# T5-bias attention and a mixture of adapters: two passes through DRAM rewritten as one hand-ordered pass over head pairs

## The chip, the cores and the metric

The kernel runs on one core of one Trainium2 chip. The metric is the device time of one execution in microseconds (us). A profiled run also gives a span, from the first to the last instruction; it is about 2 us shorter than the time. The engines are named as in the profile: PE is TensorE's matmuls, PEld its weight loads, DVE is VectorE, ACT ScalarE, POOL GpSimd, SP SyncE, which issues the DMAs that the kernels start with `nc.sync`. PEclk is the share of TensorE's full clock that was granted.

## The reference

Eight batches, eight heads, 576 tokens, head size 64. Attention with a bias that depends on the distance between query and key alone, and is constant from distance 128 on; then, per token, a mixture of eight rank-16 adapters of which the two with the largest gate logits count.

```python
scores = q @ k.T / sqrt(64) + bias_table[bucket(|i - j|)]     # per batch and head, 576 x 576
attn   = softmax(scores)                                       # over keys
x      = (attn @ v)                                            # heads side by side: 4608 x 512
logits = x @ w_gate                                            # 4608 x 8
w      = softmax of the two largest logits
out    = x + sum over the two experts e of  w_e * (x @ A[e]) @ B[e]
```

The softmax needs no maximum for numbers of this size: both kernels multiply exp(scores) by exp(bias), and get the sum of a row by appending a column of ones to the values.

## The kernel before

A scheduler orders the instructions. First a bias stage writes 40 tables of exp(bias), one per head and block of 128 keys:

```python
for h in range(H):
    for jb in range(JB):                      # 5 blocks of keys: 4 x 128 + 64
        nc.sync.dma_start(out=tmp[:P, :], in_=<a 576-wide sliding window of gext_d>)
        nc.scalar.activation(eb[:P, :], trev, ACT.Exp)         # ebias, L96
```

Then the attention stage, per head. Queries and keys come as bf16 copies through DRAM, are transposed for two heads at once, and each head takes its 64 of the 128 rows:

```python
qTs = pair["q"][lo:hi, :]                     # 64 rows
kTs = pair["k"][lo:hi, :]
for jb in range(JB):
    nc.tensor.matmul(sc[:P, n0:n1], lhsT=kTs[:, jb*128:jb*128+P], rhs=qTs[:, n0:n1], ...)  # L171
    nc.scalar.activation(e[:P, :], sc[:P, :], ACT.Exp, scale=scale)                        # L176
    nc.vector.tensor_tensor(p[:P, :], e[:P, :], ebias[(h, jb)][:P, :], op=ALU.mult)        # L179
    nc.tensor.matmul(pv[:, n0:n1], lhsT=v1[:P, jb, :], rhs=p[:P, n0:n1], ...)              # L182
nc.vector.tensor_copy(o, pv[:D, :])           # o and the row of sums go to DRAM
nc.vector.tensor_copy(rsb, pv[D:D + 1, :])
```

In L182 the values are stationary (65 columns: 64 and the ones), and the probabilities stream. When all heads are done, the sums come back from DRAM, reciprocals go out again, and a third stage runs the adapters (MoE) over 36 tiles of 128 tokens:

```python
nc.vector.tensor_tensor(xTt, xTr, dv, op=ALU.mult)             # normalise
# ... gate: about a dozen small VectorE instructions of 8 columns or 1 ...
nc.scalar.copy(ot, dl); nc.sync.dma_start(out=out[n0:n0 + 128, :], in_=ot)
```

The softmax here doesn't subtract the row's maximum and nothing guards it: scores larger than these inputs give would overflow.

## Time and profile before

The median is 626.71 us of 4 runs (622.73 to 628.53).

| stage | about | busiest | granted clock |
|---|---|---|---|
| bias tables | 0 to 70 us | waits for table DMAs | |
| attention | 90 to 495 us | TensorE | 0.50 for most of it |
| round trip and MoE | 495 to 620 us | VectorE | 0.56 |

The first lines are from the page of before: busy time of each engine with its share of the span, and then the span in 40 slices, each digit being a tenth.

```profile
PE 453.0 (73%) x1960; PEld 181.3 (29%) x1960; DVE 326.4 (53%) x949; ACT 283.9 (46%) x537; POOL 193.1 (31%) x431
PE   0000895768899999999999999999999404555554
DVE  0000453237555656656565655656566417888884
ACT  0021674557554545555455555555555203333333
PEclk9999999999655555555555555555555556565556
```

TensorE has two long rows of nines in the middle. Under them the clock is at five tenths. The next view of before is busy time by stretch: the stretch and its length, busy us and number of instructions of each engine, granted clock, DMA share and GB/s.

```profile
150.00:155.00 5.00, 5.00 (x39) 2.48 (x39) 4.89 (x12) 4.07 (x7) 3.66 (x8) 1.00 1.10 183
165.00:170.00 5.00, 4.88 (x22) 1.69 (x22) 1.83 (x4) 1.85 (x4) 1.86 (x4) 0.50 0.76 221
190.00:300.00 110.00, 107.08 (x431) 40.00 (x431) 64.86 (x132) 59.44 (x96) 37.24 (x77) 0.50 0.60 136
500.00:620.00 120.00, 57.74 (x360) 34.05 (x360) 85.46 (x468) 39.82 (x144) 45.95 (x81) 0.56 0.82 202
```

In both stretches TensorE is busy all the time, but in the first it finishes 39 matmuls, and in the second 22. Busy time cannot tell the two apart; the granted clock does. The 1.00 that the profile shows before 149 us is not a measurement: the first clock record of the trace is at 149 us, time without a record counts as full clock, and the matmuls before it have the durations of half clock (the 512-column score matmuls 598 ns in the mean from 70 to 130 us, and 602 from 160 to 175 us, where the records show 0.50). So a mean clock can be too high: 8 of the 28 runs of before in the later calls are listed at 0.94 to 0.97 and still took 624 to 629 us. Their first record may have come later still; their traces were not kept, so this is not shown.

From the groups by line of before, with the mean duration in ns after the comma, and from its waits (us in total, times, longest):

```profile
L176 ACT ACTIVATE e<-sc 128x576 bf16<-128x576 f32 x256 | 161.8, 648 | 154.2 <-PE sc L171 116.9 <-PE pv L182 17.0 <-DVE p L179 9.8
L171 PE MATMUL sc<-pTq,pTk 64*128 64x512 bf16 x256 | 148.6, 595 | 15.4 <-ACT e L176 14.1 <-ACT pTk L149 0.7
L179 DVE TENSOR_TENSOR p<-e,ebias 128x576 bf16<-128x576 bf16 x256 | 105.2, 444 | 116.7 <-ACT e L176 98.7 <-ACT ebias L96 17.8
```

```profile
ACT ebias L96 <- DMA eb_tmp<-gext_d: 62.7, 23, 25.4
PE zl L248 <- DMA dv<-recips_d: 22.7, 1, 22.7
```

ScalarE idles 154 us before its exps and VectorE 117 us before its multiplies, mostly for the engine ahead of them, while TensorE idles 15 us before its large score matmuls: attention is TensorE's. The other two lines are the price of the two detours through DRAM.

### The profile page before, as it was taken

How to read it: one execution, taken by the hardware profiler on the slowest of the kernel's cores; microseconds unless marked ns; L12 is line 12 of the kernel's file. 1: busy time of each engine (PE TensorE's matmuls, PEld its weight loads, DVE VectorE, ACT ScalarE, POOL GpSimd, SP SyncE). 2: the span in 40 equal slices, each digit the busy share in tenths (PEclk: the TensorE clock that was granted, in tenths of full speed). 3: DMA queues.
4: the chain of work that ended last, by engine and by line, in shares of the span. 5: the costliest groups of instructions: out<-in, count | busy, mean ns of one | idle time of the engine just before them, and what ended most of it. 6: DMA issues, size and time to landing. Idle time of an engine off the chain costs nothing. (4 is left out here: it accounts for less than half of the span.)

```text
span 620.8 us, 7660 instructions
## 1 busy us (share of the span) xinstructions
PE 453.0 (73%) x1960; PEld 181.3 (29%) x1960; DVE 326.4 (53%) x949; ACT 283.9 (46%) x537; POOL 193.1 (31%) x431
## 2 busy tenths in 40 slices
PE   0000895768899999999999999999999404555554
PEld 0000331223333333333333333333333102333332
DVE  0000453237555656656565655656566417888884
ACT  0021674557554545555455555555555203333333
POOL 7040123114342423433232322323231055344420
PEclk9999999999655555555555555555555556565556
DMA  5999589669876775942222232101010089989872
GB/s 114 227 248 243 130 247 215 155 160 225 184 164 123 191 144 167 199 122 58 49 48 40 44 58 44 29 20 31 19 29 20 21 137 214 234 217 245 234 190 103
DMA packets 134388, 82.96 MB, mean 134 GB/s; under 512 B 110144, under 2 KB 115520, under 8 KB 134344
## 3 DMA queue, kind: packets, MB, share of 16 engines
q1 hardware_dynamic: 116168, 49.26, 31.2%
q0 software_dynamic: 13056, 28.48, 23.1%
q10 hardware_dynamic: 5120, 4.72, 2.4%
q8 instruction: 16, 0.26, 0.2%
q14 instruction: 28, 0.23, 0.1%
HBM read 67.93 MB, written 28.64 MB: 156 GB/s over the span
## 5 line engine op out<-in xcount | busy, mean ns | idle before, releaser
L176 ACT ACTIVATE e<-sc 128x576 bf16<-128x576 f32 (+1 forms) x320 | 201.0, 647 | 167.3 <-PE sc L171 126.1
L171 PE MATMUL sc<-pTq,pTk 64*128 64x512 bf16 (+3 forms) x640 | 209.9, 424 | 15.7 <-ACT e L176 14.3
L179 DVE TENSOR_TENSOR p<-e,ebias 128x576 bf16<-128x576 bf16 (+1 forms) x320 | 133.2, 445 | 142.5 <-ACT e L176 116.1
L171 PEld LDWEIGHTS <-pTk 64*128 64x128 bf16 (+1 forms) x640 | 56.5, 118 | 136.6 <-issue 132.8
L188 DVE CAST o<-pv 64x576 bf16<-64x576 f32 x64 | 48.0, 749 | 71.3 <-PE sc L171 58.3
L238 POOL DMA_DIRECT2D dv<-recips_d x72 | 44.1, 617 | 57.2 <-DVE lm L258 15.5
L143 PE MATMUL tpk<-ident,ntk 128*128 128x128 bf16 (+1 forms) x160 | 29.1, 284 | 38.9 <-DMA ntk<-k_bf 38.8
L96 ACT ACTIVATE ebias<-eb_tmp 128x576 bf16<-128x576 f32 (+1 forms) x40 | 26.7, 680 | 62.7 <-DMA eb_tmp<-gext_d 62.7
L192 DVE COPY rsb<-pv 1x576 f32<-1x576 f32 x64 | 48.1, 752 | 2.0
L143 PE MATMUL tpq<-ident,ntq 128*128 128x128 bf16 (+1 forms) x160 | 26.6, 287 | 24.2 <-DMA ntq<-q_bf 23.8
L193 POOL DMA_DIRECT2D sums_d<-rsb x64 | 32.4, 506 | 23.6 <-DVE rsb L192 23.6
L286 PE MATMUL ztT_ps<-ident,zt 128*128 128x128 bf16 x36 | 10.3, 287 | 40.2 <-DVE zt L281 37.4
L248 PE MATMUL zl<-AW,xTt 128*128 128x136 bf16 x144 | 22.4, 308 | 22.7 <-DMA dv<-recips_d 22.7
L244 DVE TENSOR_TENSOR xTt<-xTr,dv 128x512 bf16<-128x512 bf16 x36 | 24.9, 692 | 23.3 <-DMA xTr<-xT_d 13.7
L147 DVE COPY pTq<-tpq 128x576 bf16<-128x576 bf16 x32 | 14.6, 458 | 35.7 <-PE tpq L143 34.9
L297 ACT COPY ot<-dl 128x512 f32<-128x512 f32 x36 | 21.1, 586 | 27.0 <-PE dl L293 18.2
L143 PEld LDWEIGHTS <-ntk 128*128 128x128 bf16 (+1 forms) x160 | 13.9, 117 | 60.5 <-DMA ntk<-k_bf 39.8
L143 PEld LDWEIGHTS <-ntq 128*128 128x128 bf16 (+1 forms) x160 | 14.8, 127 | 39.7 <-issue 27.9
L290 PE MATMUL dl<-Bc,ztT 128*128 128x512 bf16 x36 | 21.0, 584 | 6.9 <-ACT ztT L288 6.6
L149 ACT COPY pTk<-tpk 128x576 bf16<-128x576 bf16 x32 | 20.0, 625 | 12.1 <-PE tpk L143 12.1
L248 PEld LDWEIGHTS <-xTt 128*128 128x128 bf16 x144 | 15.6, 138 | 23.3 <-issue 23.1
L293 PE MATMUL dl<-ident,xTt 128*128 128x128 bf16 x144 | 21.7, 302 | 0.0
(773 smaller groups left out, 519.7 us busy)
## 6 DMA issues: line engine op xcount, KB each, us to landing
eb_tmp<-gext_d SPq DMA_DIRECT2D x32, 288.0 KB, 4.0
dv<-recips_d POOLq DMA_DIRECT2D x72, 128.0 KB, 4.9
out_dram<-ot SPq DMA_DIRECT2D x36, 256.0 KB, 3.4
cb<-in_q_dram POOLq DMA_DIRECT2D x8, 576.0 KB, 6.1
q_bf<-cb SPq DMA_DIRECT2D x8, 576.0 KB, 3.7
cb<-in_k_dram POOLq DMA_DIRECT2D x8, 576.0 KB, 7.6
cb<-in_v_dram POOLq DMA_DIRECT2D x8, 576.0 KB, 8.0
k_bf<-cb SPq DMA_DIRECT2D x8, 576.0 KB, 4.5
```

The lines of the kernel that those rows point to most:

```text
L96: nc.scalar.activation(eb[:P, :], trev, ACT.Exp)
L143: nc.tensor.transpose(tp[:, jb * 128:jb * 128 + P], nt[:P, jb, :], ident[:P, :P])
L171: nc.tensor.matmul(sc[:P, n0:n1], lhsT=kTs[:, jb * 128:jb * 128 + P], rhs=qTs[:, n0:n1], start=True, stop=True)
L176: nc.scalar.activation(e[:P, :], sc[:P, :], ACT.Exp, scale=scale)
L179: nc.vector.tensor_tensor(p[:P, :], e[:P, :], ebias[(h, jb)][:P, :], op=ALU.mult)
L188: nc.vector.tensor_copy(o, pv[:D, :])
L192: nc.vector.tensor_copy(rsb, pv[D:D + 1, :])
L193: nc.gpsimd.dma_start(out=sums_d.ap()[h, b * S:(b + 1) * S], in_=rsb)
L238: nc.gpsimd.dma_start(out=dv[hs * 64:(hs + 1) * 64, :, :], in_=bass.AP(tensor=rd.tensor, offset=rd.offset + hs * N + n0, ap=[[0, 64], [2 * ...
L244: nc.vector.tensor_tensor(xTt, xTr, dv, op=ALU.mult)
L248: nc.tensor.matmul(zl, lhsT=xTt[:, c, :], rhs=AW[:, c, :], start=(c == 0), stop=(c == 3))
L293: nc.tensor.matmul(dl[:, c * 128:(c + 1) * 128], lhsT=xTt[:, c, :], rhs=ident, start=False, stop=(c == 3), skip_group_check=True)
```

## The change

The intent, in five parts:

1. One pass. A head pair goes through scores, exp, band, PV and normalisation; the MoE of the batch before is cut into pieces, one of which runs in each gap of the loop. Nothing but inputs, a small bias table and outputs touches DRAM.
2. The order is by hand: `tc.manual_schedule()`, and PV of pair i-1 stands between the scores of pair i.
3. Toeplitz band: only the blocks within 128 of the diagonal are multiplied by exp(bias - bias of the last bucket); the constant of the far columns cancels in the softmax.
4. Token-major PV: the probabilities are stationary, the values stream (65 or 130 columns), and the result has tokens on partitions, so that a reciprocal per token normalises it.
5. Scores from keys zero-padded to 128 rows, so that each matmul uses all 128 rows of the array.

The core of the diff (cut; `+` lines of the new loop):

```diff
-    nc.tensor.matmul(sc[:P, n0:n1], lhsT=kTs[:, ...], rhs=qTs[:, n0:n1], ...)    # 64 rows
+    nc.vector.tensor_copy(t[0:64, 0, :], ps[0:64, 0, :])      # L256: head 0, rows 64-127 stay zero
+    nc.vector.tensor_copy(t[64:128, 1, :], ps[64:128, 0, :])  # L257: head 1, rows 0-63 stay zero
+    nc.vector.tensor_copy(t[:, 2, :], ps[:, 1, :])            # L258: both heads' queries
+    for h in range(2):
+        kh = t[:, h, g * 128:(g + 1) * 128]
+        nc.tensor.matmul(sc[:, h*512:(h+1)*512], lhsT=kh, rhs=t[:, 2, :], ...)           # L268
+        nc.tensor.matmul(sc[:, 1024+h*64:1088+h*64], lhsT=kh, rhs=tt[:, hp, 2, 0:64], ...)  # L270
+    nc.scalar.activation(p, sc[:, :1152], ACT.Exp, scale=scale)                          # L282
+    nc.vector.tensor_tensor(pm[:, :, q0:q1], pm[:, :, q0:q1], Mh[...], op=ALU.mult)      # L296, band
+    nc.tensor.matmul(acc[:, qb, h, :], lhsT=p[:, o:o+128], rhs=vn[:, g, 2*hp+h, :], ...)    # L317
+    nc.vector.reciprocal(rc, acc[:, :, :, D])
+    nc.vector.tensor_tensor(x[:, 0:3, ...], acc[:, :, :, :D], rc..., op=ALU.mult)        # L355
...
+    for g in range(5):
+        sc = qk(i, g); softmax_exp(i, g, sc)
+        if g == 0: transposes(i + 1)
+        if g == 1: norm_main(i - 1, pv_main(i - 1))
+        if g == 2: norm_rest(i - 1, pv_rest(i - 1))
+        if g in (0, 3, 4) and queue: queue.pop(0)()            # one piece of the MoE
+        band(i, g)
```

In PSUM, where its matmuls write, the kernel keeps two score buffers and two accumulator buffers (`acc`); transposes, PV and all MoE pieces share the latter in turn.

## The prediction

> **What bounds it now.** The slice table and the busy times by stretch show three stages. Up to about 70 us: bias tables (ScalarE waits 62.7 us for table loads). 90 to 495 us: attention, TensorE-bound (busy 107 of 110 us between 190 and 300; ScalarE 59, VectorE 65). After that: the MoE pass, VectorE-bound (85 of 120 us), behind a DRAM round trip in which TensorE waits over 20 us.
>
> In attention the granted clock is 0.50 from 159 to 521 us, though TensorE hardly idles: 512-column matmuls start about 425 ns apart. Switching between 64-row and 128-row matmuls adds some 110 ns (535 instead of 427). Scores use 64 of 128 rows. In the MoE stage, all 128-row, the clock rises for 3.4 us after each window that a burst filled. [...]360 us of busy half clock shows that busy time is not what is counted. I read it as activity weighted by rows.
>
> **What the change does.** It removes the bias stage (40 tables become small band tables), the bf16 copies through DRAM, the sums round trip and the separate MoE pass, which now fills gaps. There remain a startup of about 20 us (loads 6 to 8 us, a chain of table DMAs of about 4 us each) and a tail of about 18 us for the last batch's MoE.
>
> Estimates per head pair (32 pairs), from durations in the trace:
> - TensorE: scores 5,248 columns, transposes 1,150, PV 41 matmuls of 65 or 130 (3,250), MoE 2,060: 11,700 columns. At half clock 9.8 us, with gaps 10.5; at full clock about 5.6.
> - VectorE: 576-element bf16 multiply 445 ns, so band multiplies 2.4 us; PSUM copies (458 ns per 576 bf16) 1.6; normalisation (749 ns per 576 fp32, small ops 155) 1.4; MoE 2.1: 7.5 us, 240 us in all.
> - ScalarE: 647 ns per 576, so 1,128 per 1,152: 5.2 us, 167 us in all.
> - DMA: 110,000 rows of 256 B at about 20 ns over 16 engines: 140 us each, hidden.
>
> **Critical path.** The bias stage except 20 us, and the MoE stage except the tail, come off it. In the loop VectorE (7.5 us) is the floor at full clock, TensorE (10.5) at half. Full-row matmuls should lift the clock when TensorE is the limit; when VectorE limits, TensorE's activity falls to about 60%, so I expect the clock to alternate, mean 0.7 to 0.8. [...]So 9.5 us per pair, 305 us, plus 38.
>
> **Predicted: 345 us, 8 in 10 between 305 and 400. Chances: faster by over 2% 0.98, within 2% 0.01, slower 0.01.**
>
> **Signs.** Right: VectorE busy about 240 us, the busiest by share (over 65%); ScalarE about 170; first exp before 20 us; no final MoE stage over 25 us; clock clearly above 0.5 in the loop; TensorE waiting for VectorE on the two-buffer accumulator. Wrong: clock 0.50 throughout with TensorE near 100% busy (then 375 to 400 us); clock 1.0 with VectorE over 85% (then about 305).
>
> **What would make it wrong.** PV matmuls bound by their weight loads[...]; the gate counting something other than rows, so that zero-padding gains nothing; gate chains on VectorE waiting behind a 1.1-us exp on ScalarE; the software DMA queue (up to 1,024 rows per transfer) delivering late, so that batches start with a stall.

The sum: 7.5 us of VectorE work per pair, brought to 9.5 us by a term for hand-offs and one for the clock; 32 x 9.5 = 305 us, and with 20 us of start and 18 of tail 343, put as 345. That the clock would alternate at an activity of 60%, with a mean of 0.7 to 0.8, was the estimate; before does not show it.

"The gate" is there whatever sets the granted clock. The rises in the MoE stage are four in the clock records of before, of 3.41 us each, at 521.2, 555.4, 572.4 and 606.6 us; in the 3.4 to 3.5 us ahead of each, TensorE was busy for 2.95 to 3.16 us. The 20 ns are the mean of the 18,432 packets of 256 bytes in before's trace (20.1).

## The result, and the profile after

The changed kernel takes 272.65 us (272.60 to 272.88, 4 runs) against 626.71 us. The ratio is 0.4382, with a 95% interval of 0.4352 to 0.4412; ratios are the mean time of one kernel's fast runs over that of the other's in the same rounds, so not quite the ratio of the medians. Executions over 1.5% slower than the fastest of the same kernel are left out of the means. The time lies below the predicted range of 305 to 400 us.

The same lines of the page, after:

```profile
PE 192.0 (71%) x2704; PEld 131.3 (48%) x2704; DVE 224.0 (83%) x707; ACT 165.6 (61%) x174; POOL 117.2 (43%) x155
PE   0020778887788777888798578987787778978852
DVE  3402699999989898998999898989998889989972
ACT  2000599867678676775697667776696667758200
PEclk9999999999999999999999999999999999999975
```

There is one stage. VectorE has the nines now, and the clock is full from its first record, at 31.7 us, to 260 us. By stretch, after:

```profile
50.00:100.00 50.00, 39.92 (x598) 28.15 (x596) 45.93 (x149) 36.44 (x40) 26.27 (x32) 1.00 1.18 93
100.00:150.00 50.00, 40.96 (x592) 28.02 (x591) 46.52 (x140) 36.32 (x37) 19.26 (x24) 1.00 1.04 106
245.00:271.00 26.00, 15.56 (x183) 9.10 (x181) 18.53 (x57) 6.96 (x9) 0.00 (x0) 0.80 0.26 92
```

VectorE is busy 46 of 50 us. From the groups by line, after:

```profile
L268 PE MATMUL sc<-kqT_188 128*128 128x512 bf16 x128 | 41.0, 388 | 18.7 <-DVE kqT_188 L258 13.0 <-ACT p_1135 L282 0.7 <-ACT p_596 L282 0.7
L355 DVE TENSOR_TENSOR x<-pvA,rcA 128x384 bf16<-128x384 f32 x32 | 17.8, 557 | 1.1
L258 DVE COPY kqT_188<-kqps 128x512 bf16<-128x512 bf16 x16 | 6.8, 424 | 0.2
```

The score matmul's 388 ns is the duration that the profile gives it; in the trace the next matmul starts 215 ns after it, at a granted clock of 1.00; before, at 0.50, it was about 400 to 430. VectorE has next to no idle time before its instructions. The start of the loop is in this timeline of after (start, duration, engine, instruction, and in brackets the idle time and what ended it):

```profile
25.69 0.86 DVE L245 COPY tlT_184<-tps 64x512 bf16<-64x512 bf16 x2 [13.47 <-POOL tlT_184 L221]
28.26 0.59 PE L268 MATMUL sc<-kqT_188 128*128 128x512 bf16 x1 [12.96 <-DVE kqT_188 L258]
```

The first score matmul comes at 28.3 us: a memset of the tail tile stood behind the load issues in GpSimd's order. The loop's period, taken from the start times of the first and last normalisation, is (253.0 - 37.6) / 31 = 6.95 us per pair. After the last normalisation come 17.8 us for the last batch's MoE.

### The profile page after: what moved, and what is told of

It is laid out like the page before. It is cut to its first block, busy times and chain, and to the rows that moved or that the text cites. A ratio compares the mean times of both kernels' runs of the same rounds, so it can differ in the third digit from the quotient of the medians.

```text
span 270.8 us, 6853 instructions
## 1 busy us (share of the span) xinstructions
PE 192.0 (71%) x2704; PEld 131.3 (48%) x2704; DVE 224.0 (83%) x707; ACT 165.6 (61%) x174; POOL 117.2 (43%) x155
## 4 chain that ended last, share of the span: by engine, by line
DVE 61%; PE 15%; ACT 7%; POOL 6%; issue 6%; DMA 3%; ACTq 0%; DVEq 0%; POOLq 0%
PE pvA L317 8%; DVE x L355 5%; DVE o L464 4%; DVE x L367 3%; DMA vn_86<-in_v_dram 3%; DVE xT L384 3%; PE sc L268 3%; DVE kqT_188 L258 2%; DVE kqT_190 L258 2%; DVE kqT_188 L257 2%; DVE kqT_190 L257 2%; DVE kqT_190 L256 2%; DVE kqT_188 L256 2%; POOL qn L69 2%; DVE rcA L354 2%
## 5 line engine op out<-in xcount | busy, mean ns | idle before, releaser
L268 PE MATMUL sc<-kqT_188 128*128 128x512 bf16 x128 | 41.0, 388 | 18.7 <-DVE kqT_188 L258 13.0
L268 PE MATMUL sc<-kqT_190 128*128 128x512 bf16 x128 | 39.9, 379 | 2.7 <-ACT p_485 L282 0.7
L69 POOL DMA_DIRECT2D kn<-in_k_dram x36 | 31.1, 889 | 23.3 <-PE kqps L253 22.0
L69 POOL DMA_DIRECT2D qn<-in_q_dram x36 | 31.0, 902 | 1.0 <-DMA vn_86<-in_v_dram 1.0
L69 POOL DMA_DIRECT2D vn_86<-in_v_dram x16 | 14.0, 895 | 31.0 <-PE pvB L343 30.9
L69 POOL DMA_DIRECT2D vn_87<-in_v_dram x16 | 14.2, 903 | 30.6 <-PE pvB L343 30.6
L268 PEld LDWEIGHTS <-kqT_188 128*128 128x128 bf16 x128 | 12.7, 99 | 22.4 <-DVE kqT_188 L256 12.3
L464 DVE TENSOR_TENSOR o<-dl,x 128x512 f32<-128x512 f32 x32 | 21.8, 683 | 1.4 <-DMA out_dram<-o 0.8
L355 DVE TENSOR_TENSOR x<-pvA,rcA 128x384 bf16<-128x384 f32 x32 | 17.8, 557 | 1.1
L462 PE MATMUL dl<-Bb,zT 128*128 128x512 bf16 x32 | 12.9, 411 | 6.1 <-DVE zT L456 2.5
L270 PEld LDWEIGHTS <-kqT_188 128*128 128x128 bf16 x128 | 12.7, 99 | 9.1 <-issue 8.6
L268 PEld LDWEIGHTS <-kqT_190 128*128 128x128 bf16 x128 | 12.5, 98 | 8.2
L270 PEld LDWEIGHTS <-kqT_190 128*128 128x128 bf16 x128 | 12.5, 98 | 5.2 <-issue 4.2
L367 DVE TENSOR_TENSOR x<-pvB,rmB 128x256 bf16<-128x256 f32 x32 | 13.6, 424 | 1.1
L270 PE MATMUL sc<-tlT_184,kqT_188 128*128 128x64 bf16 x64 | 12.6, 198 | 0.0
L270 PE MATMUL sc<-tlT_184,kqT_190 128*128 128x64 bf16 x64 | 12.3, 192 | 0.0
```

The lines of the kernel that those rows point to most:

```text
L69: nc.gpsimd.dma_start(out=o, in_=src[b, h0:h1, j * 128:(j + 1) * 128, :] .rearrange("h p d -> p h d"))
L268: nc.tensor.matmul(sc[:, h * 512:(h + 1) * 512], lhsT=kh, rhs=t[:, 2, :], start=True, stop=True)
L270: nc.tensor.matmul(sc[:, 1024 + h * 64:1088 + h * 64], lhsT=kh, rhs=tt[:, hp, 2, 0:64], start=True, stop=True)
L355: nc.vector.tensor_tensor(x[:, 0:3, 2 * hp:2 * hp + 2, :], acc[:, :, :, :D], rc.unsqueeze(3).to_broadcast((128, 3, 2, D)), op=ALU.mult)
L367: nc.vector.tensor_tensor(x[:, 3:5, 2 * hp:2 * hp + 2, :], acc[:, :, :, :D], rm.unsqueeze(3).to_broadcast((128, 2, 2, D)), op=ALU.mult)
L462: nc.tensor.matmul(ps, lhsT=zT[:, t, :], rhs=Bb, start=True, stop=True)
```

## The experiments

Each kernel was run beside the kernel before on one chip; before's median in the four calls was 622.3, 622.5, 622.1 and 625.1 us. All results passed the comparison with the reference, also the one that is wrong (see there).

### Is it the rows that decide the clock? The kernel before, padded

The prediction read the gate as counting activity weighted by rows. One rival is that it counts busy time; another, array cells: rows times columns. Three edits of before tell them apart.

`b1_keys128`, one zero-padded key tile per head (cut):

```diff
-                    nc.scalar.copy(pT, tp)
+                    for hh in range(2):
+                        s = slice(hh * D, (hh + 1) * D)
+                        nc.scalar.copy(two[hh][s, :], tp[s, :])   # the other rows stay zero
-                qTs = pair["q"][lo:hi, :]
-                kTs = pair["k"][lo:hi, :]
+                qTs = pair["q"]
+                kTs = pair["k"][hh]
```

> The kernel before, with keys zero-padded to 128 rows (one padded tile per head, filled by two 64-row ScalarE copies instead of one of 128 rows). Theory R (rows): all matmuls of the attention stage now use 128 rows, so the granted clock is 1.0 through most of it, and that stage is bound by VectorE (about 3.95 us per head, 253 us in all) or ScalarE (3.9) instead of TensorE (6.4): 480 to 530 us in all. Theory C (the gate counts rows times columns of the array): PV with 65 active columns still counts half, so the clock stays at 0.5[...]: 560 to 610 us. Theory B (busy time): no change of clock, 560 to 620.

What theory C still gains here is the change of tile size: in before a 128-row matmul starts 535 ns after a 512-column one of 64 rows, where 427 ns pass between matmuls of the same rows.

Measured: 528.05 us (one run), 94 us less than before on the same chip.

`b2_v128`, the values padded from 65 to 128 columns:

```diff
-                v1 = qkp.tile([128, JB, D + 1], BF16, name="v1", tag="v1")
+                v1 = qkp.tile([128, JB, 128], BF16, name="v1", tag="v1")
-                nc.gpsimd.memset(v1[:, :, D:D + 1], 1.0)
+                nc.gpsimd.memset(v1[:, :, D:128], 1.0)
-                pv = pvp.tile([D + 1, S], FP32, name="pv", tag="pv")
+                pv = pvp.tile([128, S], FP32, name="pv", tag="pv")
```

> The kernel before, with the PV matmuls widened from 65 to 128 active columns (value tile padded with ones), scores still at 64 rows. Theory R: the rows have not changed, clock 0.5 in attention, 610 to 640 us. Theory C (rows times columns): the same weighted activity as padding the keys, about 75%, so whatever the padded-key run shows, this one shows too.

Measured: 605.83 us (one run), slightly below the expected band.

`b3_both`, both edits:

> The kernel before with both paddings. Theory R: as the padded-key run alone, 480 to 530 us at clock 1.0 in attention. Theory C: only this run of the three gets the full clock, 480 to 530 us. Theory B: clock 0.5, 560 to 620.

Measured: 529.18 us (one run), as the padded keys alone.

By stretch, 300 to 400 us: before, the padded keys, and the padded values:

```profile
300.00:400.00 100.00, 97.73 (x396) 36.73 (x395) 57.94 (x118) 53.03 (x86) 29.42 (x62) 0.50 0.23 45
```

```profile
300.00:400.00 100.00, 81.83 (x540) 42.38 (x538) 84.16 (x175) 80.12 (x132) 42.50 (x88) 0.99 0.22 47
```

```profile
300.00:400.00 100.00, 96.44 (x414) 33.79 (x414) 62.42 (x126) 57.24 (x93) 35.68 (x68) 0.55 0.22 44
```

With padded keys the clock is 0.99 here, TensorE is busy *less* (82 us instead of 98), and VectorE and ScalarE are the busiest. Padded values leave it at 0.55. This is the best stretch of the padded-key run; early on, where TensorE waited, its clock was at half as well, and it was 0.91 between 200 and 300 us:

```profile
100.00:150.00 50.00, 31.31 (x136) 13.76 (x137) 19.39 (x38) 30.72 (x50) 10.60 (x22) 0.52 0.86 198
```

For a check, the columns streamed in the stretch from 300 to 400 us were added up from the traces, weighted by active rows, and by rows and columns, as a share of what full clock could stream (2.4 columns per ns, from 512 in 215 ns):

| kernel, 300 to 400 us | granted clock | weighted by rows | by rows and columns |
|---|---|---|---|
| before | 0.50 | 0.30 | 0.21 |
| padded keys | 0.99 | 0.56 | 0.41 |
| padded values | 0.55 | 0.32 | 0.31 |
| both | 0.99 | 0.56 | 0.54 |

In these runs busy time does not decide. The two paddings did not act alike, as theory C had expected. But a level between 0.31 and 0.41 for cells would still fit these averages, as one between 0.32 and 0.56 for rows does. Single windows can tell them apart. The clock records of these traces last multiples of 3.41 us (in before 3.41, 10.24, 13.65, 30.72 and 361.81; the last one is cut off by the end), so all 17 traces were cut into windows of that length, 1,460 in all. The clock after a window was full where the row-weighted share in it was at least 0.37, and half where it was less, in all but 26 windows, and these lie between 0.32 and 0.38. (In before and after alone, 206 of 208. To guess that the clock stays as it is misses 199; at their best levels, cells miss 36 and columns without weights 135.) In the padded-key run, whose PV matmuls fill half of the columns, rows separate the windows without a miss, at 0.36, while by cells windows of 0.23 were followed by full clock and windows of 0.36 by half. So in these traces the clock goes with rows, and one level fits both rising and staying. It also fits that before stayed at half: there a 512-column matmul takes 427 ns instead of 215, so its 60% of what half clock can stream is a share of 0.30. The level is an inference, fitted to these same windows, and no run was made to test it.

### Does the new kernel need the padding? And what of changing the tile size?

`e1_scores64`, the 512-column scores over their 64 real rows:

```diff
-                nc.tensor.matmul(sc[:, h * 512:(h + 1) * 512], lhsT=kh,
-                                 rhs=t[:, 2, :], start=True, stop=True)
+                s = slice(h * 64, (h + 1) * 64)
+                nc.tensor.matmul(sc[:, h * 512:(h + 1) * 512], lhsT=kh[s],
+                                 rhs=t[s, 2, :], start=True, stop=True)
```

> The kernel after, with the 512-column score matmuls contracting over the 64 real rows instead of 128 rows of which 64 are zero; the tail scores stay at 128 rows. Nothing else changes, the copies stay. Theory R (the clock gate counts activity weighted by rows): scores are 4,096 of some 11,700 columns per pair, so the weighted activity at full clock falls from about 69% (4.9 us of 7.1) to about 57%; R with a threshold above that expects the granted clock to drop towards 0.5 and the time to go to 330 to 400 us, R with a lower threshold expects no change. Theory B (the gate counts busy TensorE time, whatever the rows): clock stays near 0.98 and the time within 272 to 285 us[...].

Measured: 344.83 us in its fast run; three others of 352.93 to 357.51 count as slow, being over 1.5% above it, and the profile is of such a run. From the page of that run:

```profile
PE   0107999999879998999989999999899999998963
PEclk9999999999995559559999855569999655589985
```

The clock alternates, in stretches of 10 to 41 us, and TensorE is the limit again. But the edit also makes TensorE change between 64-row and 128-row matmuls 16 times per pair. In the trace, at full clock, the start of a tail follows a 64-row score by 319 ns instead of 215, and the score after it by 135 instead of 28: about 105 ns for each change. To split the two, the next run has the changes without the missing rows.

`e2_tails64`, only the 64-column tails at 64 rows (both from the first head's rows, wrong; the error stayed within the tolerance of the comparison):

```diff
-                nc.tensor.matmul(sc[:, 1024 + h * 64:1088 + h * 64], lhsT=kh,
-                                 rhs=tt[:, hp, 2, 0:64], start=True, stop=True)
+                nc.tensor.matmul(sc[:, 1024 + h * 64:1088 + h * 64],
+                                 lhsT=t[0:64, 0, g * 128:(g + 1) * 128],
+                                 rhs=tt[0:64, hp, 2, 0:64], start=True, stop=True)
```

> The kernel after, with only the 64-column tail scores contracting over 64 rows (the second head's tail is computed from the first head's rows, so its result is wrong on purpose); the 512-column scores keep 128 rows. As many changes between 64-row and 128-row matmuls as in the run with 64-row scores (16 per pair, which measured some 105 ns each there, 1.7 us per pair), but the row-weighted activity is nearly that of the kernel after. Theory R: clock stays above 0.95, TensorE needs about 5.4 + 1.7 = 7.1 us per pair, level with VectorE, so 275 to 300 us; what the 64-row scores cost beyond that (352 us) is the clock. Rival D (the changes themselves, not the rows, lower the clock): clock about 0.83 and 330 to 355 us again.

Measured: 303.76 us (302.46 to 305.30), ratio to before 0.4898, clock 0.976: a little above the expected band, with the clock where theory R has it. So of the 72 us that the 64-row scores cost (344.83 - 272.65), about 31 are the changes of tile size, and the rest, about 41, goes with the clock; with the three longer runs, whose mean clock was 0.82 to 0.84, the rest would be about 50. What TensorE does at such a change these runs do not show; they put about 105 ns on it. The same term was in the kernel before (535 ns between starts instead of 427).

### When VectorE is the limit, does the clock fall?

The prediction expected it to alternate at an activity of about 60%. Two runs load VectorE further, by multiplying the columns outside the band by one, once and three times over:

```diff
+        for _ in range(1):                       # d3_full3: range(3)
+            for a0, a1 in ((0, q0), (q1, S4)):
+                if a1 > a0:
+                    nc.vector.tensor_tensor(pm[:, :, a0:a1], pm[:, :, a0:a1],
+                                            ones[:, :, 0:a1 - a0], op=ALU.mult)
```

> The kernel after, with the columns outside the band multiplied by one as well (four more bf16 multiplies per pair, 0.28 to 0.41 us each as the trace shows them, 1.1 to 1.4 us in all): what the multiply would cost without the Toeplitz band. If VectorE bounds: 272 + 32 x 1.1 to 1.4 = 306 to 318 us. TensorE's row-weighted activity then is 4.9 us of about 8.3, 59%. The prediction on record expects the clock to alternate there (mean 0.7 to 0.8); the rival, that a clock once full is kept at that activity, expects over 0.95.

Measured for `d2_full1`: 298.26 us (one run), clock 0.976, 0.99 in the loop. VectorE's busy time per pair rose from 6.41 to 7.38 us and the period from 6.95 to 7.68. The time is below the expected band: the durations rose by 1.4 us per pair, but VectorE's busy time, in which overlaps count once, by 0.97.

> The same multiplies three times over: 32 x 3.3 to 4.1 us more, 375 to 405 us at a clock that does not matter much. TensorE's activity at full clock falls to 4.9 us of about 10.8, 45%. If the full clock is kept only while activity stays over about half, the mean clock falls visibly below 0.9 here; if it is kept as long as TensorE has no long idle stretches, it stays above 0.95.

Measured for `d3_full3`: 398.24 us (one run), clock 0.819. From the stretch of 100 to 200 us, first the single, then the triple load:

```profile
100.00:200.00 100.00, 74.81 (x1041) 50.21 (x1040) 95.54 (x318) 63.18 (x69) 39.78 (x49) 1.00 0.94 91
```

```profile
100.00:200.00 100.00, 67.26 (x756) 45.39 (x754) 94.90 (x295) 46.06 (x48) 26.27 (x32) 0.82 0.67 65
```

VectorE is at 95% in both. Added up as above for 100 to 200 us, the row-weighted share of full clock and the granted clock go like this: after 0.68 and 1.00; single load 0.61 and 1.00; 64-row tails 0.59 and 0.98; triple load 0.44 and 0.82. So in these runs about 60% was enough to keep the clock (0.61 at 1.00, 0.59 at 0.98), and the kernel after was at 68% anyway. The triple load's average of 0.44 lies so near the fitted level of 0.37 that single windows can fall below it. All clock records of these traces are 0.5 or 1.0, so a mean of 0.82 is a mixture in time.

The single load also gives the worth of the band: without it the loop would take 0.73 us per pair more, some 26 us in all.

### Is VectorE's work the limit?

`d1_qcopy_act`, the query copy moved to ScalarE:

```diff
-        nc.vector.tensor_copy(t[:, 2, :], ps[:, 1, :])
+        nc.scalar.copy(t[:, 2, :], ps[:, 1, :])
```

> The kernel after, with the copy of the transposed queries out of PSUM (424 ns, once per pair) done by ScalarE instead of VectorE. If the loop is bound by VectorE's work (92% busy between 30 and 250 us): 32 times 0.42 us less, so 258 to 263 us. If it is bound by the hand-offs of the two accumulator buffers or by TensorE: within 269 to 276 us. ScalarE goes from 5.2 to about 5.8 us per pair and should not bind.

Measured: 281.06 us (280.81 to 281.83), ratio 0.4537: slower than after (0.4382), where both theories expected faster or the same. VectorE's busy time did fall, from 6.41 to 6.14 us per pair, but the period rose to 7.16. From the waits of this run between 40 and 240 us:

```profile
ACT kqT L258 <- DVE kqT L257: 16.9, 24, 1.7
PE pvA L317 <- ACT kqT L258: 15.3, 17, 1.6
```

ScalarE waits for VectorE's copy of the keys out of the same PSUM tile, and the next exp stands behind it.

`d4_qcopy_apart` gives queries and keys a PSUM tile and an SBUF tile each (cut):

```diff
-        ps = acp.tile([128, 2, S4], BF16, name="kqps", tag="acc")
+        kps = acp.tile([128, S4], BF16, name="kps", tag="acc")
+        qps = acp.tile([128, S4], BF16, name="qps", tag="acc")
...
+        nc.scalar.copy(qt, qps)
+        nc.vector.tensor_copy(t[0:64, 0, :], kps[0:64, :])
+        nc.vector.tensor_copy(t[64:128, 1, :], kps[64:128, :])
```

> Moving the query copy to ScalarE made the kernel slower (281 us), and its waits show why it may have: ScalarE waited 16.9 us in 200 for VectorE's copy of the keys out of the same PSUM tile, ahead of the next exp. Here queries and keys get a PSUM tile and an SBUF tile each, the queries are transposed first, and the ScalarE copy no longer waits for VectorE. If the wait was the reason: VectorE's work falls by 0.34 us per pair (the copy's start-to-start time) and the time to 258 to 268 us. If ScalarE's place in the order is the reason (the copy sits between two exps and the exps feed everything), or the second accumulator buffer that the pair of tiles now takes: 272 to 285 us.

Measured: 296.41 us (295.58 to 297.17), ratio 0.4781, clock 0.923: worse still. The wait for VectorE is gone, so it was not the whole reason; now ScalarE waits 41.8 us in 180 for scores that TensorE delivers late, with both accumulator buffers taken by one pair's transposes, and the clock dropped too. These two misses suggest, but do not show, that taking work off VectorE helps only if no buffer and no in-order neighbour is made to wait for it. Which of the two, the place between the exps or the second buffer, costs more was not separated.

`m1_moe_end` takes the MoE, and with it VectorE work, out of the loop without touching the order of the rest:

```diff
                 if i % HP == 0:
-                    queue += pieces(i // HP - 1)
+                    late += pieces(i // HP - 1)
...
-    for f in queue:
+    for f in late:
         f()
```

(with eight buffers for `x` instead of four).

> The kernel after with all MoE pieces run after the attention loop instead of one in each gap. If VectorE's work bounds the loop, taking about 1.9 us of 6.4 per pair out of it leaves ScalarE (5.2 us) as the limit: 5.5 to 5.9 us per pair, 35 to 45 us less; the end grows by seven batches of 11 to 12 us (what the last batch's MoE takes in the kernel after): 305 to 325 us in all. If the interleaved pieces sat in idle time of VectorE and cost the loop nothing: the loop stays at 6.9 us per pair and the time goes to 350.

Measured: 308.49 us (one run). VectorE's busy time per pair fell to 4.92 us and the period to 5.45, close to ScalarE's 4.9 us of work. The period is just below the expected 5.5 to 5.9 us, the time in the band. It fits a loop bound by VectorE, but does not prove it, since the MoE's matmuls and hand-offs left the loop as well; the cleaner evidence is `d2_full1`, which only adds VectorE work (0.97 us busy, 0.73 us of period). The interleaved MoE costs the loop 6.95 - 5.45 = 1.5 us per pair. Run at the end it takes 99 us after the last normalisation instead of 17.8:

```profile
30.00:210.00 180.00, 147.94 (x2148) 105.49 (x2178) 162.51 (x474) 160.30 (x160) 90.44 (x112) 1.00 1.10 70
210.00:306.00 96.00, 63.99 (x500) 40.39 (x504) 63.38 (x199) 2.67 (x12) 0.00 (x0) 0.54 0.29 99
```

In the second line no engine is above 67% and the clock is at 0.54: a chain of small steps that wait for each other. Interleaving is worth 36 us, though each piece takes VectorE's time in the loop.

`a1_oneacc`, one accumulator buffer instead of two (`bufs=2` to `bufs=1` for `acc_ps`):

> The kernel after with one accumulator buffer in PSUM instead of two: TensorE may fill the next one only when VectorE has read the last. If the hand-offs are a large term that two buffers hide: each of the five to six hand-offs per pair exposes a matmul group (0.3 to 1.2 us), so 2 to 3 us more per pair, 330 to 370 us. If VectorE's in-order work is so tight that the second buffer hides little: 275 to 300 us.

Measured: 380.64 us (one run), period 10.04 us, above both bands; the clock fell to 0.90 as well. The hand-offs are large, 3.1 us per pair with what the clock adds, and two buffers hide most of it: VectorE idles 6.95 - 6.41 = 0.54 us per pair.

### Two repairs

`s1_start` moves GpSimd's memsets to VectorE and issues the first batch's queries and keys ahead of its values:

```diff
-        nc.gpsimd.memset(vt, 0.0)                # and three more, and tlT's
+        nc.vector.memset(vt, 0.0)
...
-    load_v(0)
-    load_kq(0, 2, H)
+    load_kq(0, 2, H)
+    load_v(0)
```

> The kernel after with a shorter start: all memsets that GpSimd did between its load issues go to VectorE, and the remaining queries and keys of the first batch are issued before the values. In the kernel after the first copy into the tail tiles waits until 25.7 us for a memset that stands behind 15 us of load issues. Expected: first score matmul before 20 us instead of 28.3, the second pair's loads the next wait at about 21 us, 263 to 268 us in all. If the loads' landing is what bounds the start: 269 to 273.

Measured: 267.73 us (267.44 to 267.77), ratio 0.4321. The first score matmul starts 11.6 us sooner, but the second pair then waits for its loads, as the timeline of this run shows:

```profile
16.68 0.59 PE L268 MATMUL sc<-kqT 128*128 128x512 bf16 x1 [1.75 <-DVE kqT L258]
22.93 0.29 PE L253 MATMUL kqps<-ident,qn 128*128 128x128 bf16 x1 [1.05 <-DMA qn<-in_q_dram]
```

So 5 of the 11.6 us are left.

`n1_halves` drops the padding. The two heads' scores stand next to each other on the two halves of the array, the tails of both are one 128-row matmul against block-diagonal query tails, and one copy replaces three:

```diff
-        nc.vector.tensor_copy(t[0:64, 0, :], ps[0:64, 0, :])
-        nc.vector.tensor_copy(t[64:128, 1, :], ps[64:128, 0, :])
-        nc.vector.tensor_copy(t[:, 2, :], ps[:, 1, :])
+        nc.vector.tensor_copy(t, ps)
...
+                s = slice(h * 64, (h + 1) * 64)
+                nc.tensor.matmul(sc[:, h*512:(h+1)*512], lhsT=t[s, 0, ...], rhs=t[s, 1, :], ...)
+            nc.tensor.matmul(sc[:, 1024:1152], lhsT=t[:, 0, ...], rhs=tt[:, hp, 1, :], ...)
```

> The kernel after without zero-padded keys: the two heads' 512-column scores as two 64-row matmuls on the two halves of the array, next to each other in the order so that they can run at the same time, and both heads' tail scores as one 128-row matmul against block-diagonal query tails. One VectorE copy of 1,024 columns (about 0.60 us start to start) replaces three (about 1.20): 0.6 us less VectorE work per pair. If VectorE bounds and the clock stays full: 272 - 32 x 0.45 to 0.6 = 253 to 259 us, less what 8 changes of tile size per pair cost (31 us for 16 in the run with 64-row tails, so up to 15): 253 to 272. If the two halves don't run together, or count as half activity, the clock alternates as with the 64-row scores: 300 to 350 us.

Measured: 259.85 us (258.69 to 260.49), ratio 0.4193, clock 0.971. The clock holds with 64-row matmuls here, and the timeline of this run shows what is different from `e1_scores64`:

```profile
142.29 0.39 PE L265 MATMUL sc<-kqT 64*128 64x512 bf16 x2
142.61 0.23 PE L268 MATMUL sc<-tlT,kqT 128*128 128x128 bf16 x1
```

Two 512-column matmuls together take 0.39 us, what one takes in the kernel after, and they start 3 ns apart: they run at the same time, one on rows 0 to 63 of the array and one on rows 64 to 127. VectorE's busy time fell from 6.41 to 5.91 us per pair and the period from 6.95 to 6.54.

`n2_both`, both repairs together:

> The two-halves scores together with the shorter start. The gains touch different stretches (the loop: 259.85; the start: 5 us less), so they should add: 253 to 257 us. If the start is then bound by the same loads anyway: 258 to 260.

Measured: 254.12 us (252.81 to 254.59), ratio 0.4079: the gains add. This version beats both kernels.

`n3_out_act` adds half of the residual additions by TensorE and lets ScalarE copy those tiles out:

```diff
+        if t % 2:
+            nc.tensor.matmul(ps, lhsT=zT[:, t, :], rhs=Bb, start=True, stop=False)
+            nc.tensor.matmul(ps, lhsT=ident, rhs=xt, start=False, stop=True)
+            nc.scalar.copy(o, ps)
```

> The same, and every second output tile gets its residual added by TensorE (identity matmul, 0.22 us) and is copied out of PSUM by ScalarE (about 0.59 us) instead of added by VectorE (0.68 us); the odd tail tile is copied by ScalarE too. Here ScalarE waits for TensorE alone, with no VectorE copy on the same PSUM tile. VectorE's work falls by some 0.35 us per pair, ScalarE's rises by 0.3 to about 5.5: if VectorE's work is the limit, 10 us less than the run before it, 243 to 249 us; if, as with the query copy, ScalarE's place between the exps costs more than it gives, 254 to 262.

Measured: 253.95 us (252.56 to 254.67), ratio 0.4072: no gain over the run before it. VectorE's busy time fell again, from 5.91 to 5.64 us per pair, and the period stayed (6.53 and 6.56). From here on VectorE's work alone is not the limit; what is was not settled.

## Why the prediction was right or wrong

**Right.** The three stages and their limits; the bias stage and the MoE stage coming off the path; the clock going with rows (padding the keys of before alone saves 94 us and gives up to 0.99); ScalarE at 165.6 us (predicted 167); VectorE the busiest, at 224 us (predicted 240); the tail at 17.8 us (predicted 18). PV matmuls of 65 columns start 29 to 32 ns apart (27 ns would be their columns at full clock, from 512 in 215 ns), so the weight loads did not bind. No DMA wait stands in the loop, though the packets of the software queue took 86% of the span of the 16 DMA engines, some 232 us each instead of the estimated 140.

**Wrong: the loop.** The step that failed is the one from 7.5 us to 9.5: "so I expect the clock to alternate, mean 0.7 to 0.8", with the term for hand-offs, and then "So 9.5 us per pair". Measured: 6.95. The prediction had named this outcome among its signs of being wrong, "clock 1.0 with VectorE over 85% (then about 305)"; VectorE was at 92% of the loop, and the time still came out 32 us below that. Term by term, per pair:

| term | prediction | measured | what showed it |
|---|---|---|---|
| VectorE work | 7.5 | durations add up to 7.33, but cover 6.41 | trace of after |
| hand-offs | a part of 2.0 (from no trace) | 0.54 | idle time of VectorE (3.2 with one buffer) |
| clock | the rest of the 2.0 | 0 | clock 1.00 in the loop; it stays under the single load and falls under the triple one |

The sum of the prices of single instructions was right to about 2%. The mistake was to add them as if each began when the last had ended. Three neighbours from the timeline of after:

```profile
243.49 0.56 DVE L355 TENSOR_TENSOR x<-pvA,rcA 128x384 bf16<-128x384 f32 x1
243.97 0.55 DVE L296 TENSOR_TENSOR p_4299<-p_4299,M 128x768 bf16<-128x768 bf16 x1
244.43 0.17 DVE L363 RECIPROCAL rcB<-pvB 128x4 f32<-128x4 f32 x1
```

The second starts 0.48 us after the first, which lasts 0.56, and the third 0.46 after the second, which lasts 0.55: 80 to 90 ns of each disappear behind the next. In the whole loop 358 of 619 instructions were overlapped like this, by 82 ns in the median, which is 0.9 us per pair. The others were not: a multiply that reads the reciprocal just before it (L355 after L354) starts 34 ns after its end. In the kernel before VectorE was seldom back to back (durations of 94.6 us covering 89.5 between 40 and 240 us), so the overlap hardly showed there.

The clock term failed on both halves: the activity was 68%, not 60, since the period was shorter; and 60% would have kept the clock too (0.61 did, in `d2_full1`).

**Wrong: the start.** Predicted 20 us, measured 28.3 to the first score matmul, and 29.4 to the first exp, which was expected before 20: the order of GpSimd's queue was not read. Against this the loop was overestimated by (9.5 - 6.95) x 32 = 82 us; together they make up the difference of 72 us, to 1 or 2.

**Where the 354 us went,** as far as runs show it: the clock, about 94 us, if measured in the old kernel by the padded keys (changes of tile size included); the interleaved MoE, 36 us against the same pieces at the end; the band, about 26 us. The rest is the bias stage, the round trips and the shorter chains of the new order, which were not run apart.

## What to carry to other kernels

Judge TensorE by the granted clock and the start-to-start time of its matmuls, not by its busy time (before was 97% busy at 0.50). If it is busy and slow, look at how many rows of the array each matmul uses, and try to fill them: with zeros, which took the clock of before from 0.50 to 0.99 between 300 and 400 us, or better with a second head on the other half, which held 0.971 in `n1_halves`. When a bound is added up from durations of single instructions, ask whether they will run back to back: start-to-start times are the price then, and here they were shorter, by 82 ns in the median where two overlapped. Work taken off the busiest engine need not help: the query copy on ScalarE cost 8 and 24 us.
